# Window attention with sink columns and two feed-forward layers on one core: operands arranged on the host, transposes left out, small products on GpSimd, stages reordered

## The chip, the cores and the metric

The kernel runs on one NeuronCore of a Trainium2 chip. The metric is device time in microseconds (us) of one execution. Engines are named as in the profile: PE (TensorE matmuls), PEld (its weight loads), DVE (VectorE), ACT (ScalarE), POOL (GpSimd) and SP (SyncE, which issues the loads and stores).

## The reference, cut

```python
scores = 0.125 * q @ k.T                 # B=2, H=8, S=768, D=64
keep   = (pos_k < n_sink) | (0 <= pos_q - pos_k < window)     # 4 sinks, window 128
a      = softmax(where(keep, scores, -1e9))
x      = (a @ v) as [1536, 512]
x      = ((x @ w_a) * (x @ w_b)) @ w_out        # d_ff 1536
y      = relu(x @ w_in2)**2 @ w_out2            # d_ff 2048
```

The feed-forward weights are float64 and reach the kernel as pairs of 32-bit words. The kernel keeps nearly float32 precision in the large products: each operand is split into a high and a low part, and a product is three matmuls (high·high, low·high, high·low).

## The kernel before, in words

**Attention** works on 24 groups g: batch b (2), block i of 128 queries (6), and half m of the heads (4 heads). A group needs the key block of its own position, the one before, and 8 sink columns. `attention_fast` is a software pipeline: in step g of its main loop each stage named in the list `ORDER` runs for group g plus the stage's lag, so one step touches up to five groups. Inside that loop the instructions stay in the order in which they are written on PE, DVE, ACT and POOL (`manual_schedule`), so `ORDER` is the order of every engine's queue. The stages, with the lines where they issue:

- `pt`, `kq`: PE transposes two key and two query tiles of the next group (L233), ACT copies them out of PSUM (L239), POOL copies the sink columns of a first block (L241).
- `scores`: 4 matmuls (L258, written as 8 instructions in the profile).
- `soft0`, `soft1`: DVE picks the right key block (L271) and adds the mask with a running minimum (L274), two heads each; `exp0`, `exp1`: ACT's exponentials with their sums (L282).
- `rec`: DVE's sum and reciprocal (L287, L288), which begin a step's chain. `norm`: DVE scales heads 0 and 1 (L292); `normA`: ACT scales heads 2 and 3 (L297).
- `sp`: DVE writes the scaled sink columns three times (L305); `pst`: PE turns them (L336); `st`: ACT copies (L342); `sts`: DVE forms the low part of the middle copy (L347).
- `ptp`, `th`: PE turns the four heads' weights (L312), ACT copies (L316); `lu`: POOL cuts them into two triangles (L327, L329).
- `x`: 16 value matmuls and 2 for the sinks (L355, L360); `xh`, `xl`: ACT and DVE write the high and low parts (L368, L371).

**Weights.** `Weights.stages` loads one 512 KB piece (L537) and decodes it in six stages on ACT and DVE (L552 to L570): `abs`, `ts`, `stt`, `stt2`, `cast`, `lo`. The list `DECODE` says in which steps a piece begins; eleven pieces are decoded beside the attention.

**Feed-forward.** `Beside` gives PE one piece of 12 matmuls (L660, 128x512) per step through the stage `fill`, from the step in which the first 512 tokens are done. After the last step come the rest of these pieces, then blocks of 512 tokens through the remaining phases (L660 and the second product, L701), with the weight pieces decoded beside them.

**Loads.** SP issues keys and queries two groups ahead, values one group later, weight pieces as raw buffers come free (3). Sinks' values are loaded once by 24 transfers (L211) into a cleared weight buffer, and split by ACT and DVE (L216, L217) at the end of step 2 (`SINK`). `warm` runs 14 small matmuls at the start and 4 and 3 more in steps 0 and 1 (L380).

Of the kernel before, what the change touches and what calls it, by code (L numbers as in the profile page):

```python
# [28 lines left out]
    ("rec", -1), ("x", -3), ("th", -2), ("sp", -1), ("norm", -1), ("scores", 0), ("pt", 1), ("xh", -3),  # L29
    ("normA", -1), ("xl", -3), ("fm", 0), ("soft0", 0), ("fu", 0), ("stt2", -1), ("soft1", 0), ("abs", 0),  # L30
    ("pst", -1), ("kq", 1), ("st", -1), ("fill", 0), ("exp0", 0), ("sts", -1), ("ts", 0), ("cast", -1), ("stt",
    0), ("lu", -2), ("lo", -1), ("exp1", 0), ("ptp", -1)]
DECODE = [2, 6, 9, 10, 11, 12, 13, 15, 18, 20, 22]
WIDE = 9
SINK = (1, 2)
PINNED = 3
WARM0 = 14
WARM1 = {0: 4, 1: 3}
NV, NEX, NTH, NLU, NSP = 8, 3, 2, 2, 2
# [22 lines left out]
def setup(tc, cp, tp, n_sink, window):  # L62
    nc = tc.nc
    c = Attn()
    ident = tp.tile([P, P], F32, name="ident")
    make_identity(nc, ident)
    c.identr = cp.tile([P, P], F32R, name="identr")
    nc.vector.tensor_copy(c.identr, ident)
    c.ident = c.identr.bitcast(F32)

    raw = cp.tile([1, 4], I32, name="raw")
    nc.scalar.dma_start(raw[:, 0:2], n_sink.bitcast(I32).partition_broadcast(1))
    nc.scalar.dma_start(raw[:, 2:4], window.bitcast(I32).partition_broadcast(1))
# [12 lines left out]
    c.up = cp.tile([P, P], I32, name="upi")  # L86
    v.tensor_copy(c.up, c.upf)
# [3 lines left out]
    c.rel0 = tp.tile([P, P], F32, name="rel0")  # L91
    v.scalar_tensor_tensor(out=c.rel0, in0=c.upf, scalar=BIG, in1=d, op0=ALU.mult, op1=ALU.add)
    lo = cp.tile([1, 2], F32, name="lo_f")
    hi = cp.tile([1, 2], F32, name="hi_f")
    v.tensor_copy(lo, raw.bitcast(U32)[:, 0:4:2])
    v.tensor_copy(hi, raw[:, 1:4:2])
    c.par0 = cp.tile([1, 2], F32, name="par0")
    v.scalar_tensor_tensor(out=c.par0, in0=hi, scalar=4294967296.0, in1=lo, op0=ALU.mult, op1=ALU.add)
    return c


def masks(tc, cp, tp, c, ps):
# [13 lines left out]
    def out_of(o, x, limit):  # L116
        v.tensor_scalar(out=o, in0=x, scalar1=limit, scalar2=-BIG, op0=ALU.is_ge, op1=ALU.mult)


    sink = tp.tile([P, P], F32, name="sink")  # L120
    out_of(sink, c.col, c.ns)
    out_of(m0, c.rel0, c.w)
    v.tensor_tensor(out=m0, in0=m0, in1=sink, op=ALU.max)

    out_of(m2[:, 0:P], c.rel, c.w)
    v.tensor_copy(m2[:, P:SW], sink[:, 0:SK])
# [4 lines left out]
    v.tensor_copy(m1[:, P:SW], sink[:, 0:SK])  # L131
# [14 lines left out]
def attention_fast(tc, ctx, c, cp, tp, rp, q, k, v, xh, xl, beside):  # L146
# [3 lines left out]
    B, H, S, D = q.shape  # L150
    NB = S // P
# [707 lines left out]
```

## Time and profile before

| what | value |
|---|---|
| median of 3 runs | 676.22 us (676.17 to 676.25) |
| the profiled execution | 678.09 us, span of its instructions 676.4 us |
| busy, share of the span | PE 96%, PEld 78%, DVE 59%, ACT 43%, POOL 4% |
| granted TensorE clock, mean | 0.986 |
| packets of loads and stores | 65,560, of which 39,908 under 512 bytes |
| HBM read, written | 45.19 MB, 3.15 MB |

The span runs from the first to the last instruction of one profiled execution. The page cuts it into 40 slices; the chain of waits says what was waited for last; the timeline lists instructions in order of time, with the idle time before each and what ended it. Matmuls are pipelined: a matmul's duration overlaps the next one, so PE's pace is read from starts. A granted clock of 1.00 is 2.4 GHz, 0.50 is 1.2 GHz.

### The profile page before, as it was taken

To read this page: it belongs to the slowest core of one execution; us is meant where nothing else is said; L and a number is where in the kernel's file an instruction comes from. 1 tells how busy PE (TensorE), PEld (TensorE's weight loads), DVE (VectorE), ACT (ScalarE), POOL (GpSimd) and SP (SyncE) were. 2 spreads that over 40 slices of the span, in tenths; PEclk is the share of its full clock that TensorE was granted. 3 is DMA by queue.
4 is the path that set the end of the run, shared out by engine and by line. 5 is a ranking of instruction groups with operands and counts; after the bars stand their busy time and mean duration, and the time that the engine had idled before them with its cause. 6 is when DMAs were issued, how large, how long until landed. Compare 5 with 4: busy or idle time off the path is not lost.

```text
span 676.4 us, 8976 instructions
## 1 busy us (share of the span) xinstructions
PE 652.0 (96%) x3267; PEld 528.6 (78%) x3267; DVE 401.7 (59%) x950; ACT 290.7 (43%) x676; POOL 30.2 (4%) x53
## 2 busy tenths in 40 slices
PE   7578999999999999999999999999999999999996
PEld 5356877778788888888888888888888888888884
DVE  5698986762689872588641789535824232333323
ACT  6676886761444532545321446324532222222221
POOL 1131202120000000000000000000000000000000
PEclk9697999999999999999999999999999999999999
DMA  5853543310164550045400043200200000001011
GB/s 136 197 121 85 145 123 85 85 33 0 63 188 133 165 169 1 32 150 162 155 1 0 32 125 125 94 0 32 63 0 1 0 1 0 1 1 62 23 40 68
DMA packets 65560, 48.99 MB, mean 72 GB/s; under 512 B 39908, under 2 KB 60388, under 8 KB 65508
## 3 DMA queue, kind: packets, MB, share of 16 engines
q1 hardware_dynamic: 65504, 48.34, 24.8%
q8 instruction: 27, 0.44, 0.3%
q14 instruction: 25, 0.20, 0.1%
q10 hardware_dynamic: 4, 0.00, 0.0%
HBM read 45.19 MB, written 3.15 MB: 71 GB/s over the span
## 4 chain that ended last, share of the span: by engine, by line
PE 92%; DVE 4%; ACT 1%; DMA 1%; SPq 1%; issue 0%; DVEq 0%; ACTq 0%
PE psa L660 48%; PE acc L701 34%; PE x L355 3%; PE sc L258 3%; PE pt L233 1%; PE ptp L312 1%; ACT ex L282 1%; PE x L360 1%; DMA qraw<-in_q_dram 1%; SPq L211 1%; DVE ex L274 1%; DVE ex L292 1%; DVE sc L271 1%; PE psw L380 1%; DVE xl L371 0%
## 5 line engine op out<-in xcount | busy, mean ns | idle before, releaser
L660 PE MATMUL psa<-xh,wh 128*128 128x512 f32 x480 | 188.9, 393 | 0.8 <-DVE gs L677 0.8
L660 PE MATMUL psa<-xh,wl 128*128 128x512 f32 x480 | 187.0, 390 | 0.0
L660 PE MATMUL psa<-xl,wh 128*128 128x512 f32 x480 | 186.8, 389 | 0.0
L660 PEld LDWEIGHTS psa<-xh,wh 128*128 128x128 f32 x480 | 90.4, 188 | 19.8 <-DVE gs L677 1.3
L660 PEld LDWEIGHTS psa<-xh,wl 128*128 128x128 f32 x480 | 90.1, 188 | 19.0
L660 PEld LDWEIGHTS psa<-xl,wh 128*128 128x128 f32 x480 | 90.3, 188 | 18.3
L740 DVE TENSOR_TENSOR g<-u 128x512 f32<-128x512 f32 x48 | 33.1, 690 | 111.2 <-ACT u L730 111.2
L730 ACT ACTIVATE u<-psa 128x512 f32<-128x512 f32 x48 | 28.7, 598 | 119.0 <-PE psa L660 119.0
L701 PE MATMUL acc<-wh,gl 128*128 128x512 f32 x192 | 74.7, 389 | 0.0
L701 PE MATMUL acc<-wl,gh 128*128 128x512 f32 x192 | 74.7, 389 | 0.0
L58 ACT CAST gh<-g 128x512 fp32r<-128x512 f32 x72 | 44.6, 620 | 64.7 <-DVE g L740 34.8
L552 ACT ACTIVATE wtmp<-wraw 128x512 f32<-128x512 f32 x68 | 45.5, 672 | 54.0 <-DMA wraw<-in_moe_w_in_dram 17.9
L59 DVE TENSOR_TENSOR gl<-g,gh 128x512 fp32r<-128x512 f32 x72 | 49.6, 689 | 31.2 <-ACT gh L58 30.9
L701 PE MATMUL acc<-wh,gh 128*128 128x512 f32 x192 | 62.7, 389 | 0.0
L568 ACT CAST wh<-wtmp 128x512 fp32r<-128x512 f32 x68 | 41.8, 618 | 35.5 <-DVE wtmp L563 15.5
L570 DVE TENSOR_TENSOR wl<-wtmp,wh 128x512 fp32r<-128x512 f32 x68 | 46.5, 685 | 17.0 <-ACT wh L568 15.9
L701 PE MATMUL acc<-gl,wh 128*128 128x512 f32 x144 | 56.0, 389 | 0.0
L701 PE MATMUL acc<-gh,wl 128*128 128x512 f32 x144 | 55.9, 389 | 0.0
L560 DVE SCALAR_TENSOR_TENSOR wtmp<-wraw,wtmp 128x512 int32<-128x512 int32 x68 | 47.4, 699 | 0.6
L701 PE MATMUL acc<-gh,wh 128*128 128x512 f32 x144 | 47.3, 389 | 0.0
L563 DVE SCALAR_TENSOR_TENSOR wtmp<-wraw,wtmp 128x512 int32<-128x512 int32 x68 | 46.5, 684 | 0.2
L701 PEld LDWEIGHTS acc<-wl,gh 128*128 128x128 f32 x192 | 36.1, 188 | 7.5
(92 smaller groups left out, 753.4 us busy)
## 6 DMA issues: line engine op xcount, KB each, us to landing
wraw<-in_moe_w_out_dram SPq DMA_DIRECT2D x28, 512.0 KB
wraw<-in_moe_w_in_dram SPq DMA_DIRECT2D x16, 512.0 KB
wraw<-in_moe_w_a_dram SPq DMA_DIRECT2D x12, 512.0 KB
wraw<-in_moe_w_b_dram SPq DMA_DIRECT2D x12, 512.0 KB
vraw<-in_v_dram SPq DMA_DIRECT2D x24, 128.0 KB
out_dram<-part SPq DMA_DIRECT2D x12, 256.0 KB
kraw<-in_k_dram SPq DMA_DIRECT2D x23, 128.0 KB
qraw<-in_q_dram SPq DMA_DIRECT2D x23, 128.0 KB
```

The costliest lines, as they stand in the source:

```text
L58: nc.scalar.copy(hi, src)
L59: (lo_eng or nc.vector).tensor_sub(lo, src, hi.bitcast(F32))
L258: nc.tensor.matmul(o, lhsT=half(flat, r)[:, qp, 0:P], rhs=y, start=True, stop=True)
L552: a = nc.scalar.activation(tf, up.bitcast(F32), AF.Abs)
L560: nc.vector.scalar_tensor_tensor(out=t, in0=up, scalar=0x3FFFFFFF, in1=t, op0=ALU.bitwise_or, op1=ALU.bitwise_and)
L563: nc.vector.scalar_tensor_tensor(out=t, in0=low, scalar=29, in1=t, op0=ALU.logical_shift_right, op1=ALU.bitwise_or)
L568: nc.scalar.copy(hi, tf)
L570: nc.vector.tensor_sub(lo, tf, hi.bitcast(F32))
L660: self.tc.nc.tensor.matmul(ps, lhsT=w[:, kt, :], rhs=x[:, kt, ts], start=n == 0, stop=n == 3 * KT - 1)
L701: mm = nc.tensor.matmul(acc[d], lhsT=a, rhs=b_, start=f == 0 and j == 0, stop=f == NF - 1 and j == 2)
L730: nc.scalar.activation(u, pa, AF.Relu)
L740: nc.vector.tensor_mul(g, u, u)
```

## The change

1. A new function `layout` rearranges inputs on the host: keys and queries come transposed, with the 8 sink keys appended to every key block; values come with all heads of a block together; the sinks' values arrive as one array `vs`; `n_sink` and `window` arrive repeated for 128 partitions; each weight piece is one contiguous block.
2. The stages `pt`, `kq` and `sts` are gone with their 96 transposes and 24 copies. Keys and queries of a block (all 8 heads) are loaded every second step.
3. `norm` scales head 0 on DVE, `normA` heads 1 and 2 on ACT, a new `normP` head 3 on POOL. `sp` is three POOL instructions: scale, round into two of three copies, difference into the third.
4. The sinks' values come in one transfer per batch, split at the end of steps 3 and 6 (`VS`). The masks need no matmul; those not used by a first block are made at the end of step 0 (`later_masks`). The warming matmuls of steps 0 and 1 are gone.
5. `ORDER` is new; of its stages, `x` now stands behind `scores`, `xl` behind `fill`. In `DECODE` the second and seventh pieces begin one step earlier.

```diff
-DECODE = [2, 6, 9, 10, 11, 12, 13, 15, 18, 20, 22]
+    ("exp1", -1), ("scores", 0), ("st", -2), ("rec", -1), ("fm", 0), ("stt", -1), ("norm", -1), ("th", -2),
...
+DECODE = [2, 5, 9, 10, 11, 12, 12, 15, 18, 20, 22]
...
-SINK = (1, 2)
+VS = (3, 6)
...
-WARM1 = {0: 4, 1: 3}
...
+    raw = cp.tile([P, 4], I32, name="raw")
+    nc.scalar.dma_start(raw, span.bitcast(I32))
...
-    nc.tensor.matmul(ps, lhsT=c.one, rhs=c.par0, start=True, stop=True)
...
+    keys = p1.tile([P, NK, H // 2, SW], F32, name="keys")
...
+    def load_kq(n, part=slice(0, H // 2)):
...
+            queries[n] = p2.tile([P, H // 2, P], F32, name="queries", tag="queries", bufs=NQ)
+        b, i = divmod(n, NB)
+        nc.sync.dma_start(keys[:, n % NK, part], k[b, i, :, part])
+        nc.sync.dma_start(queries[n][:, part], q[b, i, :, part])
...
+    with tc.high_priority(offset=1000):
+        load_kq(0, slice(0, 2))
+        load_kq(0, slice(2, 4))
+    load_kq(1)
+    load_v(0)
...
-        nc.gpsimd.memset(vsr, 0.0)
-        for kind in range(3):
-            for j in range(GH):
-                for b in range(B):
-                    p0 = (kind * GH + j) * SK
-                    nc.sync.dma_start(vsr[p0:p0 + SK, b, j // 2:H // 2:2, (j % 2) * D:(j % 2 + 1) * D],
-                                      v[b, j:H:GH, 0:SK, :].rearrange("m s d -> s m d"))
...
+    def sink_load(b):
+        vsr[b] = p1.tile([96, H // 2, P], F32, name="vsr", tag="vsr")
+        nc.sync.dma_start(vsr[b], vs_in[:, b])
...
-                nc.tensor.transpose(pt[:, j, pp], t[:, 2 * pp:2 * pp + 2, :].rearrange("t h d -> t (h d)"), c.ident)
...
-        nc.scalar.copy(kq[:, ks:qs + 1:qs - ks, :, 0:P], pts.pop(g))
...
-        nc.vector.tensor_mul(ex[:, 0:2, 0:P], ex[:, 0:2, 0:P], ss[:, 0:2].unsqueeze(2).to_broadcast([P, 2, P]))
...
+        nc.vector.tensor_scalar_mul(ex[:, 0, 0:P], ex[:, 0, 0:P], ss[:, 0:1])
...
+    def normalize_p(g):
+        ex, ss = pns[g][0:2]
+        for h in range(3, 4):
+            nc.gpsimd.tensor_scalar_mul(ex[:, h, 0:P], ex[:, h, 0:P], ss[:, h:h + 1])
...
+        sn = ex[:, :, P:SW]
+        sps[g] = sp = p2.tile([P, 3, GH, SK], F32R, name="sp", tag="sp", bufs=NSP)
+        nc.gpsimd.tensor_mul(sn, sn, ss.unsqueeze(2).to_broadcast([P, GH, SK]))
+        nc.gpsimd.tensor_copy(sp[:, 0:3:2], sn.unsqueeze(1).to_broadcast([P, 2, GH, SK]))
+        nc.gpsimd.tensor_sub(sp[:, 1], sn, sp[:, 0].bitcast(F32))
...
-        nc.vector.tensor_sub(sts[g][32:64], sps.pop((g, "t"))[32:64], sts[g][32:64].bitcast(F32))
...
+        if g == 0:
+            later_masks(tc, cp, tp, c)
             flag(tc, cp, c)
-            sink_split()
+        if g in VS:
+            sink_split(VS.index(g))
+            if g == VS[0]:
+                sink_load(1)
...
-            self.tc.nc.sync.dma_start(raw.rearrange("p (k f) t -> p k (f t)", k=src.shape[1]), src)
+            self.tc.nc.sync.dma_start(raw.rearrange("p n t -> p (n t)"), src)
```

DVE's queue, one step without weight stages, before the first feed-forward piece. `ss` holds the sums, `sc` the scores in PSUM, `ex` the exponentials. Before:

```order
L287 TENSOR_SCALAR ss<-ss 128x4
L288 RECIPROCAL ss<-ss 128x4
L305 TENSOR_TENSOR sp<-ex,ss 128x96
L292 TENSOR_TENSOR ex<-ex,ss 128x2x128
L371 TENSOR_TENSOR xl<-x,xh 128x2x128
L271 COPY_PREDICATED sc<-upi,sc 128x2x128
...
L274 ISA nb 128x1
L347 TENSOR_TENSOR st<-pst,st 32x128
```

With the change:

```order
L254 TENSOR_SCALAR ss<-ss 128x4
L255 RECIPROCAL ss<-ss 128x4
L259 TENSOR_SCALAR ex<-ex,ss 128x128
L238 COPY_PREDICATED sc<-upi,sc 128x2x128
...
L241 ISA nb 128x1
L340 TENSOR_TENSOR xl<-x,xh 128x2x128
```

The sink product, the difference and one of two heads have left the queue, and `xl` moved behind the two softmax stages.

POOL's queue in such a step; `th` holds the turned weights, `lu` their two triangles. Before:

```order
L327 AFFINE_SELECT lu<-th 128x512
L329 AFFINE_SELECT lu<-th 128x512
```

With the change:

```order
L278 TENSOR_TENSOR ex<-ex,ss 128x4x8
L279 CAST sp<-ex 128x2x32
L280 TENSOR_TENSOR sp<-ex,sp 128x32
L269 TENSOR_SCALAR ex<-ex,ss 128x128
L301 AFFINE_SELECT lu<-th 128x512
L303 AFFINE_SELECT lu<-th 128x512
```

Four short instructions of the group whose sums have just been formed now stand ahead of the two selects.

PE's queue in such a step (`pst` the turned sink columns, `ptp` the turned weights). Before:

```order
L312 MATMUL ptp<-identr,ex 128x128 x4
L355 MATMUL x<-lu,vraw 64x128 x8
L360 MATMUL x<-st,vs 128x128 x2
L258 MATMUL sc<-kq 128x272 x4
L233 MATMUL pt<-identr,kraw 128x128 x2
L233 MATMUL pt<-identr,qraw 128x128 x2
L336 MATMUL pst<-identr,sp 96x128
```

With the change:

```order
L286 MATMUL ptp<-identr,ex 128x128 x4
L225 MATMUL sc<-keys,queries 128x272 x4
L324 MATMUL x<-lu,values 64x128 x8
L329 MATMUL x<-st,vs 128x128 x2
L310 MATMUL pst<-identr,sp 96x128
```

The four transposes are gone and the scores stand ahead of the value matmuls. The first piece of 12 feed-forward matmuls stood behind `pst` of group 9, in step 10; it now stands behind `pst` of group 10, in step 11.

## Rows read from the trace of the kernel before

**Rows 1.** Windows: stretch; busy PE, PEld, DVE, ACT, POOL; granted clock, DMA share, GB/s.

```profile
5.00:10.00 5.00, 4.18 (x34) 3.05 (x33) 2.99 (x19) 2.71 (x10) 1.30 (x3) 1.00 1.03 216
...
17.00:20.00 3.00, 0.00 (x0) 0.00 (x0) 0.54 (x6) 0.00 (x0) 0.00 (x0) 0.86 0.06 14
20.00:23.00 3.00, 0.00 (x0) 0.00 (x0) 1.17 (x2) 1.82 (x4) 0.00 (x0) 0.50 0.48 106
...
100.00:120.00 20.00, 20.00 (x146) 15.65 (x145) 14.68 (x61) 14.37 (x51) 3.89 (x6) 1.00 0.38 94
```

**Rows 2.** Chain that ended last, in order of time: start, duration, engine, what.

```profile
103.75 1.12 PE sc L258 x8
105.56 2.77 PE psa L660 x12
...
110.17 1.12 PE sc L258 x8
```

**Rows 3.** Timeline, DVE: `rec` of groups 0, 2, 3, 9; start, duration, instruction.

```profile
9.64 0.17 DVE L287 TENSOR_SCALAR ss<-ss 128x4 f32<-128x4 f32 x1 [1.17 <-ACT ex L282]
...
23.14 0.17 DVE L287 TENSOR_SCALAR ss<-ss 128x4 f32<-128x4 f32 x1
...
27.84 0.16 DVE L287 TENSOR_SCALAR ss<-ss 128x4 f32<-128x4 f32 x1
...
59.22 0.59 DVE L287 TENSOR_SCALAR ss<-ss 128x4 f32<-128x4 f32 x1
```

**Rows 4.** Timeline, SP and ACT: the sinks' load and split.

```profile
9.45 10.79 SPq L211 DMA_DIRECT2D wraw<-in_v_dram  x24
...
21.18 1.14 ACT L216 CAST vs<-wraw 96x512 fp32r<-96x512 f32 x2 [4.53 <-DMA wraw<-in_v_dram]
```

**Rows 5.** Timeline, PE's weight loads: the wait for the last of the first transfers.

```profile
4.69 0.18 PEld L233 LDWEIGHTS pt<-identr,qraw 128*128 128x128 f32 x1 [0.21 <-DMA qraw<-in_q_dram]
```

**Rows 6.** Groups of instructions by line: busy us, mean ns, idle before.

```profile
L560 DVE SCALAR_TENSOR_TENSOR wtmp<-wraw,wtmp 128x512 int32<-128x512 int32 x68 | 47.4, 699 | 0.6
...
L556 DVE TENSOR_SCALAR wtmp<-wtmp 128x512 f32<-128x512 f32 x68 | 29.1, 431 | 17.6 <-ACT wtmp L552 16.8
...
L239 ACT COPY kq<-pt 128x512 f32<-128x512 f32 x24 | 13.9, 578 | 8.8 <-PE pt L233 8.7
...
L241 POOL COPY kq<-kq 128x32 f32<-128x32 f32 x4 | 1.2, 306 | 21.6 <-ACT kq L239 21.6
...
L85 DVE TENSOR_SCALAR up<-d 128x128 f32<-128x128 f32 x1 | 0.2, 232 | 0.2 <-POOL d L81 0.2
```

**Rows 7.** Timeline, DVE: one step of the front without weight stages.

```profile
37.09 0.17 DVE L287 TENSOR_SCALAR ss<-ss 128x4 f32<-128x4 f32 x1 [0.42 <-ACT ex L282]
...
37.50 0.26 DVE L305 TENSOR_TENSOR sp<-ex,ss 128x96 f32<-128x96 f32 x1
37.68 0.85 DVE L292 TENSOR_TENSOR ex<-ex,ss 128x256 f32<-128x256 f32 x1
...
40.82 0.28 DVE L347 TENSOR_TENSOR st<-pst,st 32x128 fp32r<-32x128 f32 x1
```

**Rows 8.** Timeline: a POOL select beside that product, and the product alone.

```profile
37.59 0.66 POOL L327 TENSOR_SCALAR_AFFINE_SELECT lu<-th 128x512 f32<-128x512 f32 x1 [3.01 <-ACT th L316]
...
102.74 0.42 DVE L292 TENSOR_TENSOR ex<-ex,ss 128x256 f32<-128x256 f32 x1
```

**Rows 9.** Timeline, PE: values and scores at the low clock, first feed-forward piece, transposes.

```profile
57.34 1.97 PE L355 MATMUL x<-lu,vraw 128*64 128x128 f32 x16 [1.12 <-DVE st L347]
...
59.87 2.19 PE L258 MATMUL sc<-kq 64*128 64x272 f32 x8
...
62.96 0.74 PE L660 MATMUL psa<-xh,wh 128*128 128x512 f32 x1
...
104.79 0.44 PE L233 MATMUL pt<-identr,kraw 128*128 128x128 f32 x2
...
105.29 0.27 PE L336 MATMUL pst<-identr,sp 128*96 128x128 f32 x1
```

More of the change, by code (lines that the diff above doesn't have):

```diff
@@ L28 @@
 ORDER = [
[L29 to L32, printed above, removed]
-DECODE = [2, 6, 9, 10, 11, 12, 13, 15, 18, 20, 22]
[4 rows of a table added]
+DECODE = [2, 5, 9, 10, 11, 12, 12, 15, 18, 20, 22]
 WIDE = 9
-SINK = (1, 2)
+VS = (3, 6)
 PINNED = 3
 WARM0 = 14
-WARM1 = {0: 4, 1: 3}
-NV, NEX, NTH, NLU, NSP = 8, 3, 2, 2, 2
+NQ, NV, NEX, NTH, NLU, NSP = 3, 5, 3, 2, 2, 2
+NK = 4
 T = 512
@@ L214, in sink_split @@
-    def sink_split():
-        for b in range(B):
-            nc.scalar.copy(vs[:, b], vsr[:, b])
-            nc.vector.tensor_sub(vs[64:96, b], vsr[64:96, b], vs[64:96, b].bitcast(F32))
-    kq = p1.tile([P, 6, 2, SW], F32, name="kq")
-    flat = kq.rearrange("p a c s -> p (a c) s")
+    pns, ths, sps, sts, lus, xs = ({} for _ in range(6))
+    keys = p1.tile([P, NK, H // 2, SW], F32, name="keys")
+    queries, vals = {}, {}
+    def load_kq(n, part=slice(0, H // 2)):
+        if n >= B * NB:
+            return
+        if n not in queries:
+            queries[n] = p2.tile([P, H // 2, P], F32, name="queries", tag="queries", bufs=NQ)
+        b, i = divmod(n, NB)
+        nc.sync.dma_start(keys[:, n % NK, part], k[b, i, :, part])
+        nc.sync.dma_start(queries[n][:, part], q[b, i, :, part])
@@ L224, in half, with sink_split @@
+    def sink_split(b):
+        nc.scalar.copy(vs[:, b], vsr[b])
+        nc.vector.tensor_sub(vs[64:96, b], vsr[b][64:96], vs[64:96, b].bitcast(F32))
     def half(t, r):
         return t[r * D:(r + 1) * D]
[L227 to L234 removed]
@@ L257, in scores @@
                     o = sc[:, r, 0:2 * SW].rearrange("q (u s) -> q u s", u=2)
-                nc.tensor.matmul(o, lhsT=half(flat, r)[:, qp, 0:P], rhs=y, start=True, stop=True)
+                nc.tensor.matmul(o, lhsT=half(queries[n], r)[:, 2 * m + pp], rhs=y, start=True, stop=True)
     def maxima(g, pp):
@@ L384, in attention_fast @@
                   soft1=lambda g: maxima(g, 1), exp0=lambda g: exps(g, 0), exp1=lambda g: exps(g, 1), rec=reciprocal,
-                  norm=normalize, normA=normalize_too, sp=sinks, pst=sinks_turn, st=sinks_copy, sts=sinks_low, pt=transposes, kq=transposes_copy,
-                  x=values, xh=x_high, xl=x_low)
+                  sp=sinks, pst=sinks_turn, st=sinks_copy, x=values, xh=x_high, xl=x_low,
+                  norm=normalize, normA=normalize_a, normP=normalize_p)
     warm(WARM0)
-    transposes(0)
-    masks(tc, cp, tp, c, bank("par")[:, 0, 0:2])
-    transposes_copy(0)
     for g in range(N + 3):
@@ L843, in build, with layout, pairs, blocks @@
     return nc
+def layout(inputs):
+    import numpy as np
+    def pairs(a, n):
+        B, H, S, D = a.shape
+        a = a.reshape(B, H // 2, 2, S // n, n, D).transpose(0, 3, 2, 5, 1, 4)
+        return a.reshape(B, S // n, 2 * D, H // 2, n)
+    def blocks(w, inner):
+        if inner:
+            K, FF = w.shape
+            w = w.reshape(K // P, P, FF // P, P).transpose(2, 1, 0, 3)
+        return np.ascontiguousarray(w.reshape(-1, P, 512)).view(np.int64)
+    q, k, v = (np.asarray(inputs[n]) for n in "qkv")
+    B, H, S, D = v.shape
+    out = {"q": pairs(q, P)}
+    sinks = pairs(k[:, :, 0:SK], SK)
+    out["k"] = np.concatenate([pairs(k, P), np.broadcast_to(sinks, (B, S // P, *sinks.shape[2:]))], axis=4)
+    out["v"] = v.reshape(B, H, S // P, P, D).transpose(0, 2, 3, 1, 4)
+    vs = np.zeros((3, 4, SK, B, H // 4, 2, 2, D), v.dtype)
+    for j in range(4):
+        vs[:, j, :, :, :, j // 2, j % 2] = v[:, j::4, 0:SK].transpose(2, 0, 1, 3)
+    out["vs"] = vs.reshape(12 * SK, B, H // 2, 2 * D)
+    out["span"] = np.broadcast_to(np.stack([inputs["n_sink"], inputs["window"]]).astype(np.int64), (P, 2))
+    for n in _INS[5:]:
+        out[n] = blocks(np.asarray(inputs[n]), not n.endswith("out"))
+    return out
 def kernel(**inputs):
@@ L849 @@
     from concourse.bass_utils import run_bass_kernel_spmd as _run
+    inputs = layout(inputs)
     arrays, shapes = {}, {}
```

210 lines of the change are left out of this document (76 added, 134 removed), and 3 rows, old and new, of the table ORDER.

## The prediction

> **What bounds the kernel now.** First come the windows, which cut the span into stretches by what each engine did. From the first feed-forward piece at 62.96 us [rows 9] on, PE works without a pause worth naming: 20.00 of 20 us in the stretch 100 to 120, at the full clock, with DVE and ACT at about 14.5 of 20 [rows 1]. There the chain of waits has nothing but PE's own work, step after step, from one group's scores at 103.75 to the next one's at 110.17 [rows 2], 6.42 us. So time from 62.96 to the end of the span at 676.4, 613.4 us, is a count of PE's work, and only work that leaves PE shortens it. Before 62.96 PE is not the bound: from 17 to 23 it did nothing [rows 1]. There the timeline of DVE is the thing to read, by its first instruction of each step, the `rec` of one group (group 0 at 9.64, 2 at 23.14, 3 at 27.84, 9 at 59.22) [rows 3]. I therefore sum two parts: when the first piece starts, and what PE has left then.
>
> **Part one, the front.** *Step 0.* PE waits for the last of the first four transfers until 4.69 [rows 5]. They carry 256 KB before and 553 KB now, since a block's keys and queries hold all 8 heads. At the 216 GB/s of the stretch 5 to 10 [rows 1] the extra 297 KB cost 1.4 us, so the second half lands at 6.1; scores 0.4 and two softmax instructions 0.5 bring DVE to 7.0. No transposes and no copy come between. But the later masks and the flags, some eleven small instructions, now stand ahead of `rec` of group 0: at 0.17 [rows 3] to 0.23 each [rows 6], 1.9 to 2.5 us; I take 2.0, since most write few columns. `rec` of group 0: 9.0 instead of 9.64 (bounds 7.5, if the longer transfers run faster, and 9.8).
>
> *Steps 1 and 2.* Before, `rec` of group 2 comes 13.50 us after that of group 0. Six of these, 17 to 23, are the sinks' wait: DVE did the flags (0.54) and the split (1.17) and was idle otherwise [rows 1], because 24 small transfers held SP for 10.79 us and ACT waited 4.53 for them [rows 4]. All six leave these steps. ACT's two copies of 0.578 [rows 6], on the chain here, go too: 13.50 - 6.0 - 1.1 = 6.4, so 15.4.
>
> *A step without weight stages.* DVE is busy from `rec` at 37.09 to the end of `sts` at 41.10, 4.01 us, after 0.42 idle [rows 7]. Out go the sink product (0.18, start to start), the difference (0.28), and of the norm's 0.85 all but one head, which at 0.232 for 128x128 [rows 6] leaves 0.6 saved: 1.06 to 1.1 in all, or 2.9 left. `xl` behind `soft1` covers part of the wait for ACT's exponentials, but with less DVE work that wait grows to about 0.7: 3.6 a step. ACT loses only its copy; PE needs x, scores, sinks and `ptp`, some 3.3. So three engines then stand close together, and I expect no more than this. A weight piece adds two instructions of 0.43 to one step and three of 0.70 [rows 6] to the next: 0.9 and 2.1 (the first fills the wait).
>
> *The sum.* Step 3, with the second half of a piece and a sinks' split of 0.6 to 0.7: 2.9 + 2.1 + 0.6 = 5.6, `rec` of group 3 at 21.0. From group 3 to group 9 it took 31.4 before [rows 3]; now 3.6 + 3.9 + 5.6 + 3.6 + 3.6 + 3.9 = 24.2, and 0.8 for collisions with POOL (below): 25.0, at 46.0. Step 10 carries one piece's second half and the next one's first: 2.9 + 2.1 + 0.9 = 5.9, at 51.9. The first piece now stands in step 11, a step later than before, because `xl` of group 7 falls behind `fill` in step 10. It comes behind `pst` of group 10, which waits for POOL's three new instructions: 0.3 each by POOL's 128x32 copy of 0.306 [rows 6], so 1.4 behind `rec`. First piece: 53.3.
>
> *The clock.* After the six idle microseconds the clock in the rows stood at 0.50 from 20 to 23 [rows 1]; scores then take 2.19 instead of about 1.15 [rows 2, 9]. The change removes that pause, but also the warming matmuls and the transposes, and leaves PE about 4 us of work between 4 and 13. One stretch at 1.2 GHz there is likely; the long step 3 hides most of it. I take 2.0 (0 to 6). **First piece at 55.3 instead of 62.96** (bounds 50 and 61).
>
> **Part two, PE's remaining work.** In each of steps 11 to 22 four transposes go, 0.50 from their start to `pst`'s [rows 9]: 12 x 0.50 = 6.0. Since the first piece starts a step later, one step's attention work more is already done: 6.42 - 2.75 for the piece - 0.50 = 3.2. Against that, weight stages crowd on DVE, since `DECODE` begins two pieces in step 12. Step 11: 2.9 + 2.1 + 0.9. Steps 12 and 13 serve first blocks, whose two key choices fall away (0.9, if each is as long as the 0.43 of [rows 6]): 2.0 + 2.1 + 1.8, and 2.0 + 4.2 with a feed-forward product of 0.7. With 0.3 a step for collisions that is 6.2, 6.2 and 7.2, where PE has 5.9: 1.9 us in which PE waits (0 to 6). 613.4 - 6.0 - 3.2 + 1.9 = 606.1. Everything after the attention is the same PE work. **Span 55.3 + 606.1 = 661.4.** The profiled execution took 678.1 with a span of 676.4, its median is 676.2; I take the 15.0 off the median: **661.2 us.**
>
> **What is costed at nothing.** Longer, fewer loads: PE's stretches after 63 show no wait for them, so they help only the front. The contiguous weight pieces likewise. ACT's copy beyond step 2: ACT is not the bound there. POOL was idle for 3.01 us before its select at 37.59 [rows 8]; the four new instructions, 1.2 us by the copy's 0.306, fit into that. If they took as long as a select, 0.66 [rows 8], POOL would have 3.9 a step and be as late as DVE: this is the upper bound, and it costs the front 0.3 a step.
>
> The copy's 0.306 is the nearest row for POOL, a one-input instruction; two of the new ones have two inputs, and no row shows that on POOL. The Trainium skill ("GPSIMD Engine Reference", section "Engine selection") speaks against this move: elementwise work on VectorE, since two-input operations are about twice as slow on GpSimd. By that rule the product and the difference would take about 0.6 each as an estimate, `pst` would come 0.6 later, and the sum would be 661.8 instead of 661.2.
>
> **The rivals.** *The port takes it back.* A DVE product beside a POOL select took 0.85 [rows 7, 8], alone 0.42 [rows 8]. Each new POOL instruction can meet a two-input DVE instruction so. Two more such meetings in each of about nine front steps cost 2 x 0.43 x 9 = 7.7: 669. For it: POOL's busy time per step doubles. Against it: what stays on DVE reads mostly PSUM, and the norm is a single head. The Trainium skill ("Perfetto Trace Analysis", section "Optimizing Scalar/DVE Operations") warns of this: the two engines share a port, so moving work between them might not help. Chance 0.13.
>
> *POOL becomes the bound, slower than before.* Say every step takes y because POOL does. The first piece then comes at 9.0 + 10 y + 1.4, and each of the 15 steps behind it costs y - 5.9 more, while DVE's 1.9 no longer counts. All of the 15.0 is lost when 25 y = 15.0 + 55.3 - 10.4 + 88.5 + 1.9, at y = 6.0. POOL's two selects are 1.3 of that [rows 8], so from 1.2 us for each new instruction on this decides; at 1.3 each, y is 6.5 and the time 676.2 + 25 x 0.5 = 689. The point is an instruction on 32 to 128 columns that takes four times the copy's 0.306. Chance 0.04.
>
> *PE stays at 1.2 GHz through the front.* At that clock values 1.97 and scores 2.19 [rows 9], and the sinks, `pst` and `ptp` about 2, make 6.1 a step: PE is the bound from group 3 at 21.0, seven such steps and 5.0 to the first piece, 68.7 instead of 55.3: 674.6. Against it: PE would then work without a pause, as it does from 100 to 120, where the clock is 1.00 [rows 1], so some of the seven steps would be fast; with four slow ones it is 669. Chance 0.04.
>
> *Better than forecast.* No low clock, faster first loads, no wait in steps 11 to 13: 50 + 604.2, less 0.2, is 654. Chance 0.09.
>
> **How the numbers follow.** The forecast, DVE's queue shortened and PE counted down, 655 to 667, has 0.70. The range 655 to 669 takes it in with the larger part of the port case and leaves out the end of the good case, the clock case's last third and POOL's. A measurement of this kernel tells 0.2% from no change. Only POOL's case is slower (0.04); what it gives near its point, with the clock case at its full price, is the same (0.02); the others are faster: 0.94.
>
> **What would show it.** In the changed profile: `rec` of group 2 by about 15.4 with no pause behind the sinks' load; DVE's plain step 3.6 long; the first feed-forward piece near 55; then PE full, in steps of 5.9 us. It would be wrong if the first piece stood later than 61, if POOL ended a step's last wait (its new instructions above 1.1 us), or if PE paused between pieces for weights.

## The result and the profile after

The changed kernel takes **658.76 us** (median of four runs, 658.13 to 660.43) against 676.24 in the same comparison: ratio 0.9745, interval [0.9727, 0.9763], or 17.2 us faster. The forecast was 661.2 in a range of 655 to 669. The profiled execution, the longest of the four, took 660.43 us with a span of 658.7; the rows below are from it.

The two parts of the sum share the gain: the first feed-forward piece stands at 54.11 us instead of 62.96 [rows 9], 8.9 earlier, and from there to the end it takes 604.6 us instead of 613.4, 8.8 less.

The windows of the changed kernel (stretch; busy PE, PEld, DVE, ACT, POOL; granted clock, DMA share, GB/s) answer to [rows 1]:

```profile
5.00:10.00 5.00, 2.86 (x20) 1.90 (x20) 3.84 (x30) 3.70 (x18) 0.61 (x1) 0.90 1.01 329
...
20.00:25.00 5.00, 4.30 (x24) 2.72 (x21) 4.22 (x20) 4.47 (x19) 2.74 (x7) 0.50 0.50 183
...
100.00:120.00 20.00, 20.00 (x146) 15.52 (x146) 15.96 (x60) 14.60 (x53) 8.99 (x22) 1.00 0.17 54
160.00:180.00 20.00, 18.21 (x81) 15.06 (x81) 18.13 (x35) 9.28 (x16) 0.00 (x0) 1.00 0.45 150
```

The pause of 17 to 23 is gone: DVE and ACT are busy for over four of the five microseconds from 20 to 25. Transfers move at 329 GB/s in 5 to 10, where it was 216. From 100 to 120 PE still has no pause, and POOL has 8.99 where it had 3.89. But in two of these stretches something is lost: the clock is 0.50 from 20 to 25, and PE has 1.79 us of pause in 160 to 180.

DVE's timeline, `rec` of groups 0 to 5, 9 and 10, answers to [rows 3]:

```profile
7.47 0.16 DVE L254 TENSOR_SCALAR ss<-ss 128x4 f32<-128x4 f32 x1
10.21 0.17 DVE L254 TENSOR_SCALAR ss<-ss 128x4 f32<-128x4 f32 x1 [1.20 <-ACT ex L249]
15.49 0.17 DVE L254 TENSOR_SCALAR ss<-ss 128x4 f32<-128x4 f32 x1 [0.68 <-ACT ex L249]
20.84 0.17 DVE L254 TENSOR_SCALAR ss<-ss 128x4 f32<-128x4 f32 x1
24.20 0.17 DVE L254 TENSOR_SCALAR ss<-ss 128x4 f32<-128x4 f32 x1 [0.40 <-ACT ex L249]
29.26 0.17 DVE L254 TENSOR_SCALAR ss<-ss 128x4 f32<-128x4 f32 x1 [0.35 <-ACT ex L249]
...
45.40 0.16 DVE L254 TENSOR_SCALAR ss<-ss 128x4 f32<-128x4 f32 x1
50.71 0.16 DVE L254 TENSOR_SCALAR ss<-ss 128x4 f32<-128x4 f32 x1
```

Two steps are longer than the forecast has them: the one from group 1 to group 2 lasts 5.28 us (8.02 from group 0, not 6.4), and the one from group 4 to group 5 lasts 5.06, not 3.9. What held the first is in SP's and ACT's timelines:

```profile
5.98 0.59 SPq L496 DMA_DIRECT2D wraw<-in_moe_w_a_dram  x1
...
13.22 0.68 ACT L511 ACTIVATE wtmp<-wraw 128x512 f32<-128x512 f32 x1 [1.83 <-DMA wraw<-in_moe_w_a_dram]
```

The first weight piece is issued at 5.98, as the twelfth load, and ACT waits 1.83 us for it, with the exponentials of group 2 queued behind `abs`. What held the second, and what stands ahead of the first piece, is in PE's and ACT's timelines (they answer to [rows 9]; the last three rows are a saturated step):

```profile
23.48 2.19 PE L225 MATMUL sc<-keys,queries 64*128 64x272 f32 x8
25.59 1.29 PE L324 MATMUL x<-lu,values 128*64 128x128 f32 x16
27.29 0.37 ACT L337 CAST xh<-x 128x256 fp32r<-128x256 f32 x1 [1.34 <-PE x L329]
...
49.46 0.70 PE L286 MATMUL ptp<-identr,ex 128*128 128x128 f32 x4 [1.56 <-DVE xl L340]
50.09 2.19 PE L225 MATMUL sc<-keys,queries 64*128 64x272 f32 x8
52.21 1.63 PE L324 MATMUL x<-lu,values 128*64 128x128 f32 x16
...
54.11 0.47 PE L619 MATMUL psa<-xh,wh 128*128 128x512 f32 x1
...
101.73 1.19 PE L225 MATMUL sc<-keys,queries 64*128 64x272 f32 x8
...
104.15 0.23 PE L310 MATMUL pst<-identr,sp 128*96 128x128 f32 x1
...
107.59 1.19 PE L225 MATMUL sc<-keys,queries 64*128 64x272 f32 x8
```

Twice the scores take 2.19 us, at the low clock, instead of 1.19. The values stand behind them now, so they come late; ACT's `xh` then waits 1.34 for them, and the exponentials wait behind `xh`. A saturated step lasts 107.59 - 101.73 = 5.86 us instead of 6.42 [rows 2].

POOL's timeline, the three sink instructions and the head's norm, first with little beside them; then the cast beside a weight decode on DVE, whose row stands above it:

```profile
24.75 0.24 POOL L278 TENSOR_TENSOR ex<-ex,ss 128x32 f32<-128x32 f32 x1 [0.71 <-DVE ss L255]
25.06 0.24 POOL L279 CAST sp<-ex 128x64 fp32r<-128x64 f32 x1
25.38 0.25 POOL L280 TENSOR_TENSOR sp<-ex,sp 128x32 fp32r<-128x32 f32 x1
25.61 0.60 POOL L269 TENSOR_SCALAR ex<-ex,ss 128x128 f32<-128x128 f32 x1
...
51.78 0.69 DVE L522 SCALAR_TENSOR_TENSOR wtmp<-wraw,wtmp 128x512 int32<-128x512 int32 x1
51.83 0.73 POOL L279 CAST sp<-ex 128x64 fp32r<-128x64 f32 x1
```

The pause behind the attention is PE's row at 161.87, from the list of waits along PE's timeline:

```profile
161.87 0.47 PE L619 MATMUL psa<-xh,wh 128*128 128x512 f32 x1 [1.79 <-DVE gs L636]
```

ACT had the product's input, `u`, done at 158.0, but DVE's queue has six decode instructions of three weight pieces ahead of `gs`: they start at 158.63 to 160.71, the first after 1.25 us of waiting for ACT, and `gs` follows at 161.04 (DVE's timeline).

### The profile page after: what moved, and what is told of

It is laid out like the page before. It is cut to its first block, busy times and chain, and to the rows that moved or that the text cites. A ratio compares the mean times of both kernels' runs of the same rounds, so it can differ in the third digit from the quotient of the medians.

```text
span 658.7 us, 8703 instructions
## 1 busy us (share of the span) xinstructions
PE 638.1 (97%) x3162; PEld 515.9 (78%) x3162; DVE 384.5 (58%) x908; ACT 279.1 (42%) x652; POOL 59.7 (9%) x132
## 2 busy tenths in 40 slices
DMA packets 17411, 49.47 MB, mean 75 GB/s; under 512 B 2064, under 2 KB 2576, under 8 KB 17360
## 4 chain that ended last, share of the span: by engine, by line
PE 84%; DVE 6%; DMA 4%; ACT 2%; issue 1%; POOL 1%; SPq 1%; POOLq 0%; ACTq 0%; DVEq 0%
PE psa L619 45%; PE acc L660 31%; DMA wraw<-in_moe_w_a_dram 3%; PE sc L225 3%; PE x L324 3%; DMA wraw<-in_moe_w_out_dram 1%; PE ptp L286 1%; DVE wtmp L522 1%; DVE wtmp L519 1%; PE x L329 1%; ACT wtmp L511 1%; ACT ex L249 1%; DVE ex L241 1%; DVE wl L529 1%; DVE gl L59 1%
```

## The experiments

Twelve kernels ran, in three groups, each against the kernel before on the same chip (its medians: 677.36, 676.82 and 678.10). As these differ by over 1 us, ratios are compared; 0.001 is 0.68 us. The changed kernel's is 0.9745 [0.9727, 0.9763]. The last column is read from one execution of each kernel; in which steps the clock is low differs among these (see `e10`), and such a step counts about 1.2 us.

| run | median us | ratio, interval | first piece |
|---|---|---|---|
| e1_no_gpsimd | 673.97 | 0.9957 [0.9940, 0.9975] | 61.07 |
| e2_transposes_back | 666.89 | 0.9855 [0.9837, 0.9872] | 52.89 |
| e3_before_sinks | 673.83 | 0.9955 [0.9936, 0.9975] | 59.04 |
| e4_old_order | 661.96 | 0.9772 [0.9751, 0.9792] | 52.49, a step earlier |
| e5_no_gpsimd_early | 673.18 | 0.9945 [0.9926, 0.9965] | 60.48 |
| e6_weight_first | 658.59 | 0.9733 [0.9717, 0.9750] | 51.88 |
| e7_head_pace | 659.28 | 0.9735 [0.9719, 0.9752] | 54.48 |
| e8_xl_before_fill | 657.07 | 0.9709 [0.9692, 0.9726] | 48.68, a step earlier |
| e9_three_edits | 656.61 | 0.9686 [0.9669, 0.9702] | 47.07, a step earlier |
| e10_norm_on_vector | 660.84 | 0.9750 [0.9732, 0.9768] | 53.34 |
| e11_weights_strided | 662.69 | 0.9777 [0.9757, 0.9796] | 52.15 |
| e12_warm_front | 658.72 | 0.9721 [0.9702, 0.9740] | 52.27 |

**Is it the GpSimd move?** The first run undoes it in the changed kernel.

```diff
-        nc.vector.tensor_scalar_mul(ex[:, 0, 0:P], ex[:, 0, 0:P], ss[:, 0:1])
+        nc.vector.tensor_mul(ex[:, 0:2, 0:P], ex[:, 0:2, 0:P], ss[:, 0:2].unsqueeze(2).to_broadcast([P, 2, P]))
...
-        nc.gpsimd.tensor_mul(sn, sn, ss.unsqueeze(2).to_broadcast([P, GH, SK]))
-        nc.gpsimd.tensor_copy(sp[:, 0:3:2], sn.unsqueeze(1).to_broadcast([P, 2, GH, SK]))
-        nc.gpsimd.tensor_sub(sp[:, 1], sn, sp[:, 0].bitcast(F32))
+        nc.vector.tensor_mul(sps[g], ex[:, :, P:SW].unsqueeze(1).to_broadcast([P, 3, GH, SK]),
+                             ss.unsqueeze(1).unsqueeze(3).to_broadcast([P, 3, GH, SK]))
...
+        nc.vector.tensor_sub(sts[g][32:64], sps.pop((g, "t"))[32:64], sts[g][32:64].bitcast(F32))
```

> The changed kernel with the move to GpSimd undone: the sink product (three copies), the low part of its middle copy and the norm of two heads stand on VectorE again, the norm of the other two on ScalarE; layout, loads and the order of the other stages stay as changed. Theory (VectorE's queue sets the front, PE's work the rest): VectorE gets 0.7 to 0.8 us a step back, the first feed-forward piece comes at 59 to 61 instead of 54.1, the steps behind it stay as long, time 664 to 667. Rival (the port takes back what leaves VectorE, or ScalarE and PE set the front): first piece at 53 to 56, time 658 to 660.

Both were too low: 673.97, a ratio 0.0212 above the changed kernel's, or 14.3 us. The first piece comes 7.0 later, and from 47 us on PE pauses 7.9 us in eight waits of `pst` for the product (5.6 of it in the six that lie behind the first piece), which in the new order stands late in DVE's queue. So a rival was left open, that it is the place and not the engine; `e5` puts the product straight behind `rec` (the edit against `e1`):

```diff
-    ("exp1", -1), ... ("stt", -1), ("norm", -1), ("sts", -2), ... ("x", -3), ("sp", -1), ("pst", -1),
+    ("exp1", -1), ... ("stt", -1), ("sp", -1), ("norm", -1), ("sts", -2), ... ("x", -3), ("pst", -1),
```

> As e1_no_gpsimd, but the sink product stands on VectorE straight behind the reciprocal, where the kernel before had it, and not behind the first softmax stage, where PE's turn of the sink columns and the feed-forward piece queued behind it waited for it. It tells how much of e1's 15 us is the GpSimd move and how much that place. Theory (the move is worth the 0.8 us a step of the front, and the waits behind the first piece came from the place): first piece at 60 to 61, steps behind it 5.8 to 6.0 without waits of PE, time 664 to 667. Rival (the move is worth all of it, since VectorE's longer queue delays PE behind the first piece too): 671 to 674.

673.18, which is the rival's: the place is worth 0.8 us, inside the noise, and the engine, with the form of the instructions, 13.5. The waits of PE from 47 us on show the form of it (waited for, by what: us in total, times, longest):

```profile
PE ptp L279 <- DVE xl L338: 4.6, 2, 2.7
PE x L322 <- DVE st L314: 3.6, 2, 2.3
...
```

No single instruction is waited for: PE waits twice for `xl`, behind DVE's two softmax stages, before the first piece, and twice for `st`, behind the product and the norm, after it. DVE's window shows its queue nearly full, 35.69 of 40 us, where the changed kernel has 32.05:

```profile
60.00:100.00 40.00, 37.57 (x270) 28.94 (x264) 35.69 (x130) 28.12 (x100) 6.39 (x9) 1.00 0.44 141
```

**Sinks or norm?** `e10` leaves the sinks on GpSimd and moves the head's norm back to DVE.

```diff
-            nc.gpsimd.tensor_scalar_mul(ex[:, h, 0:P], ex[:, h, 0:P], ss[:, h:h + 1])
+            nc.vector.tensor_scalar_mul(ex[:, h, 0:P], ex[:, h, 0:P], ss[:, h:h + 1])
```

> The changed kernel, but the one head's norm that GpSimd does is back on VectorE behind the other head's; the sinks' three instructions stay on GpSimd. Theory (the long cost of undoing the whole move, 14.5 us, is VectorE's queue in proportion to the busy time it gets back): the norm is about a third of it, so 663 to 665, first piece at 56 to 57 us. Rival (the cost was the sinks' product and difference, which stand between `rec` and the transposes that PE waits for, and the norm is free): 657 to 660.

The rival held, by the ratio: 0.9750 against 0.9745. DVE's timeline of one plain step shows why:

```profile
37.04 0.17 DVE L254 TENSOR_SCALAR ss<-ss 128x4 f32<-128x4 f32 x1 [0.40 <-ACT ex L249]
...
37.46 0.29 DVE L259 TENSOR_SCALAR ex<-ex,ss 128x128 f32<-128x128 f32 x1
37.66 0.28 DVE L269 TENSOR_SCALAR ex<-ex,ss 128x128 f32<-128x128 f32 x1
...
40.60 0.17 DVE L254 TENSOR_SCALAR ss<-ss 128x4 f32<-128x4 f32 x1 [0.40 <-ACT ex L249]
```

The step, `rec` at 37.04 to 40.60, lasts 3.56 us; in the changed kernel the same step (37.97 to 41.54) lasts 3.57, with a wait of 0.62 at its end. The second head's 0.2 us, start to start, goes into that slack. In `e5`, with the product, the difference and two heads on DVE, the plain step is 3.99 long (41.89 to 45.88). So it is mainly the sinks' work that had to leave DVE. How much the form of the norm adds is not shown: `e1` and `e5` do it as one two-input product of 128x256, `e10` as two scalings of 128x128. In a plain step that is 0.45 against 0.40, start to start, but where a POOL select is already under way (51.58 to 52.23 in `e5`), DVE's product takes twice as long; where the product starts first (42.48, 0.42 long), it is the select that takes 0.84 instead of 0.63 to 0.65:

```profile
42.55 0.84 POOL L294 TENSOR_SCALAR_AFFINE_SELECT lu<-th 128x512 f32<-128x512 f32 x1 [3.92 <-ACT th L283]
...
51.66 0.85 DVE L259 TENSOR_TENSOR ex<-ex,ss 128x256 f32<-128x256 f32 x1
```

`e10` also shows how far single traces can be compared. Its step from group 4 to group 5 lasts 3.85 (24.06 to 27.91), with the clock at 1.00 from 22 to 28; but its step 10 lasts 6.63 (44.46 to 51.09) instead of 5.31, since there the clock is 0.50, the values are slow and ACT's `xh` waits for them:

```profile
45.00:48.00 3.00, 3.00 (x23) 1.96 (x19) 2.82 (x11) 1.29 (x4) 2.58 (x5) 0.50 0.16 31
48.59 0.37 ACT L337 CAST xh<-x 128x256 fp32r<-128x256 f32 x1 [2.29 <-PE x L329]
```

So a first piece that comes 1 us earlier or later in one trace settles nothing, and the times of `e10` still leave the norm up to some 2 us.

**The transposes.** `e2` puts four back into each group on PE, into a PSUM bank that nothing reads, without the copies.

```diff
+            nc.tensor.transpose(pt[:, pp], keys[:, n % NK, 2 * m + pp, 0:P], c.ident)
...
+            nc.tensor.transpose(pt[:, 2 + pp], queries[n][:, 2 * m + pp], c.ident)
```

> The changed kernel with four transposes per group put back on PE alone, behind the scores; nobody reads them. Theory (behind the first piece time is a count of PE's work, in front of it PE has room): 0.5 us in each of steps 11 to 23, 6.0 to 6.5 in all, the front longer by 0 to 2 us, time 665 to 668. Rival (PE's room is there behind the first piece too, since VectorE or the weights set the pace): 659 to 661. Second rival (the extra work keeps the clock up in the front): first piece earlier than 54.1, time 663 to 665.

666.89, 0.0110 or 7.4 us more: what theory said. A saturated step in PE's timeline, from `sc` to `sc`, is 6.45 long, 0.59 above the changed kernel's:

```profile
105.17 1.19 PE L225 MATMUL sc<-keys,queries 64*128 64x272 f32 x8
106.28 0.44 PE L232 MATMUL pt<-identr,keys 128*128 128x128 f32 x2
...
111.62 1.19 PE L225 MATMUL sc<-keys,queries 64*128 64x272 f32 x8
```

Behind the first piece `e2` takes 664.7 - 52.89 = 611.8 us, 7.2 more. Yet the first piece comes 1.2 us earlier. That doesn't make the transposes free in the front: the plain step from group 7 to group 8 lasts 4.17 there (36.83 to 41.00, DVE's timeline) instead of 3.57. What comes back is clock: the step from group 4 to group 5 lasts 3.88 instead of 5.06, and the scores ahead of the first piece are fast. That is the second rival's mechanism, but `e10` and `e11` have that step fast without added work, so that the transposes keep the clock up isn't shown.

**The sinks' load.** `e3` is the kernel before with the sinks' values in one transfer.

```diff
-        for kind in range(3):
-            for j in range(GH):
-                for b in range(B):
...
+        nc.sync.dma_start(vsr, vs_in)
```

> The kernel before with one part of the change alone: the sinks' values come from the host in one transfer in place of 24 and the clearing. Theory (the stretch 17 to 23 was a wait for these transfers and for SP behind them): first piece at 56 to 58 instead of 62.96, time 669 to 671. Rival (the wait is for the bytes in front of it, keys, queries and weights, and only changes its name): 674 to 676.

673.83, or 3.0 us less, with the interval 1.7 to 4.3: less than theory said, but more than the rival. `rec` of group 2 moves from 23.14 to 18.84, 4.3 and not 6, since split and flags stay in that step, as DVE's timeline shows:

```profile
17.52 1.29 DVE L211 TENSOR_TENSOR vs<-wraw,vs 32x512 fp32r<-32x512 f32 x2
18.84 0.17 DVE L281 TENSOR_SCALAR ss<-ss 128x4 f32<-128x4 f32 x1
```

**The order.** `e4` gives the changed kernel the old `ORDER` (without the removed stages, `normP` behind `norm`) and the old `DECODE`.

```diff
-DECODE = [2, 5, 9, 10, 11, 12, 12, 15, 18, 20, 22]
+DECODE = [2, 6, 9, 10, 11, 12, 13, 15, 18, 20, 22]
```

> The changed kernel with the stages in the order of the kernel before (the removed ones left out, the new norm beside the old one) and its list of weight pieces. Theory (the sums of each engine's work set the front, the order only moves waits): first piece in step 10 again at 51 to 57, time 657 to 663. Rival (the order carries the gain: with the old one ScalarE and PE wait for GpSimd's sink chain within the step): first piece at 59 to 63, time above 665.

661.96, 0.0027 or 1.8 us above, with overlapping intervals: by their ends, at most some 4 us lie in the new order.

**The wait for the first weight piece.** `e6` asks for it at the start of step 0, ahead of the keys and queries which that step loads, and not in step 1.

```diff
+        if g == 0:
+            beside.W.load()
         if g % 2 == 0:
             load_kq(g // 2 + 2)
...
-        if step + 1 in DECODE[:2]:
+        if step + 1 in DECODE[1:2]:
```

> The changed kernel with its first weight piece asked for at the start of step 0, ahead of the third block's keys and queries, instead of in step 1 behind them. In the changed kernel ScalarE waited 1.83 us in step 2 for that piece, with the exponentials of group 2 behind it. Theory (that wait is the 1.7 us by which step 2 was longer than forecast): reciprocal of group 2 at 13.6 to 14.0 instead of 15.49, first feed-forward piece at 52 to 53, time 657 to 658. Rival (the front makes the loss up later, or keys and queries come late instead): 658.5 to 660.

The load goes out 1.9 us earlier, as the eighth, the wait of `abs` is gone (no idle time before it), and `rec` of group 2 comes at 13.31 instead of 15.49 (SP's and ACT's timelines):

```profile
4.07 0.43 SPq L498 DMA_DIRECT2D wraw<-in_moe_w_a_dram  x1
...
11.04 0.67 ACT L513 ACTIVATE wtmp<-wraw 128x512 f32<-128x512 f32 x1
```

The first piece is 2.2 us earlier in the profile, as theory said, but the time is only 0.8 less by the ratio, with overlapping intervals, and the median is the rival's. The traces are of single executions, and the changed kernel's is the longest of its four; whether all 2.2 arrive stays open.

**The wait behind the attention.** `e7` lets a decode go ahead with every second piece there, and no longer at the pace of the later pieces.

```diff
-                        W.ahead()
+                        W.ahead(2)
```

> The changed kernel with a weight piece decoded after every second feed-forward piece, instead of every third, in the stretch between the attention and the first block (124 to 160 us, where VectorE is busy for two fifths). In the changed kernel PE waited 1.79 us at 161.9 for a product that stood behind weight stages on VectorE, and the chain then goes through loads of weights. Theory (after the attention, now 21 us shorter, the weights are the next to be late): less waiting, time 657 to 658.5. Rival (that wait is the change of the PSUM pools, as in the kernel before with 0.85, and one does not get around it): 658.5 to 660.

The wait is 0.85 us instead of 1.79, but the time doesn't tell it from the changed kernel (0.9735): this cost is too small to matter alone. As the rival had it, 0.85 is left, which the kernel before has too; `e4` and `e8` come to the same without this edit.

**The wait for `xl`.** `e8` puts `xl` ahead of `fill` and `soft1`.

```diff
-    ("fu", 0), ("xh", -3), ("cast", -1), ("fill", 0), ("soft1", 0), ("xl", -3), ("lu", -2), ("ptp", -1),
+    ("fu", 0), ("xh", -3), ("cast", -1), ("xl", -3), ("fill", 0), ("soft1", 0), ("lu", -2), ("ptp", -1),
```

> The changed kernel with the low part of the value product (xl) ahead of the feed-forward piece and of the second softmax stage, so that the first piece comes in step 10 again and the PSUM buffer of the values is freed sooner for the turned weights (PE waited 2.8 us in all for it). Theory (VectorE is the front's queue: xl waits for PE's values and holds up the second softmax stage behind it): first piece 4 to 6 us earlier, but steps of the front longer by 0.3 to 0.6, time 657 to 662. Rival (the freed buffer matters more): 655 to 657.

657.07, 0.0036 or 2.4 us less, between the two expectations, and both have their part: a plain step does get longer (38.21 to 42.24, 4.03 instead of 3.57), but the buffer comes free sooner. PE's timeline: the wait for `xl` at the last step without pieces is halved, the scores behind it are fast (1.19), and the first piece stands in step 10, where it does wait for POOL:

```profile
44.76 0.66 PE L286 MATMUL ptp<-identr,ex 128*128 128x128 f32 x4 [0.77 <-DVE xl L340]
...
48.58 0.27 PE L310 MATMUL pst<-identr,sp 128*96 128x128 f32 x1 [0.51 <-POOL sp L280]
48.68 0.47 PE L619 MATMUL psa<-xh,wh 128*128 128x512 f32 x1
```

**Together.** `e9` has the edits of `e6`, `e7` and `e8`.

> The changed kernel with the edits of three earlier runs together: `xl` before `fill`, first weight piece asked for at step 0, one decode with every second feed-forward piece in the head. Theory (what comes before the first piece and the wait behind the attention add up): 1.5 us for `xl`, 0.2 to 2 for the early weight, up to 0.5 for the pace: 655 to 657, first piece before 48.7 us. Rival (the gains cancel, because the early steps are then held by another engine): 657 to 659, not to be told from the run with `xl` alone (657.07).

656.61, ratio 0.9686: 4.0 us below the changed kernel's, with intervals apart, and 21.2 below the kernel before. The time and the first piece at 47.07 are as theory said. But against `e8` the intervals overlap, so the rival isn't out.

**Contiguous weights.** `e11` leaves the weights in memory as they were; each piece is a strided load.

```diff
-            self.tc.nc.sync.dma_start(raw.rearrange("p n t -> p (n t)"), src)
+            self.tc.nc.sync.dma_start(raw.rearrange("p (k f) t -> p k (f t)", k=src.shape[1]), src)
```

> The changed kernel, but the weights lie in memory as before, so each piece is loaded in strided rows and not in one contiguous block. Theory (transfers of weights stand beside PE's work everywhere but before the first piece): 658 to 660, steps behind the first piece unchanged. Rival (the piece's longer transfer delays the decodes in step 2 and at the wait behind the attention): 661 to 664, with `rec` of group 2 over 16.5 us or the wait at `gs` over 3 us.

Not settled: the median, 662.69, is the rival's, but the runs lie between 659.19 and 663.52, and the interval overlaps the changed kernel's. In the profiled execution, the fastest of the four, nothing waits longer for weights but `abs` in step 2 (2.14 instead of 1.83), although the packets go from 17,411 to 32,771.

**The clock.** `e12` gives PE six warming matmuls in each of steps 0 to 3.

```diff
+WARM1 = {0: 6, 1: 6, 2: 6, 3: 6}
...
+        if g in WARM1:
+            warm(WARM1[g])
```

> The changed kernel with six more warming matmuls on zeros in each of steps 0 to 3, so that PE does not stand still there. Theory (the half clock in the stretch 20 to 25 costs the front 1 to 2 us): the clock in 20 to 25 rises towards 1.00, the first piece comes at 52 to 53 us and the time is 657 to 658. Rival (VectorE sets the front, and PE's low clock lies beside it): 658 to 661, first piece at 54 or later.

The granted clock is 1.00 in every stretch from 5 to 35, and the step from group 4 to 5 is 3.88 us long instead of 5.06 (DVE's and PE's timelines; the values follow at 23.63 and not at 25.59, behind fast scores):

```profile
23.53 0.17 DVE L255 TENSOR_SCALAR ss<-ss 128x4 f32<-128x4 f32 x1 [0.40 <-ACT ex L250]
23.63 1.09 PE L325 MATMUL x<-lu,values 128*64 128x128 f32 x16
...
27.41 0.16 DVE L255 TENSOR_SCALAR ss<-ss 128x4 f32<-128x4 f32 x1
```

So the low clock costs the front 1.2 us in that step, as theory said (`e10` and `e11` have it fast too, 3.85 and 3.88), and the first piece comes at 52.27. The warming holds up `rec` of group 0, to 8.75, so part is given back; the time, 658.72, is 1.6 less by the ratio, inside the interval. The other slow scores stay, at 48.35, behind the wait for `xl`; those `e8` removes.

## Why the prediction was right, point by point

The forecast's case, DVE's queue shortened and PE counted down, is what happened, and the time lies 2.4 us below it. In part that is luck: two terms of the front were off by about 1.5 us each, and cancel. The terms of the front, against DVE's rows above:

| term | forecast | measured |
|---|---|---|
| `rec` of group 0 | 9.0 | 7.47 |
| from there to group 2 | 6.4 | 8.02 |
| step 3 | 5.6 | 5.35 |
| group 3 to group 9 | 25.0 | 24.56, 1.2 of it clock |
| step 10 | 5.9 | 5.31 |
| to the first piece | 1.4, and 2.0 for the clock | 3.40, over 1 of it clock |
| first piece | 55.3 | 54.11 |

*Step 0 was mis-sized by 1.5 us.* The step "the second half lands at 6.1; scores 0.4" let group 0 wait for all of the first four transfers. Its four heads are the first part of `load_kq`, so its scores need the first two alone and start at 4.14; the second half is group 1's, whose scores wait for it till 5.89 (PE's timeline):

```profile
4.14 1.23 PE L225 MATMUL sc<-keys,queries 64*128 64x128 f32 x8
5.89 0.71 PE L225 MATMUL sc<-keys,queries 64*128 64x128 f32 x8 [0.52 <-DMA queries<-in_q_dram]
```

DVE has finished group 0's softmax at 5.9 instead of 7.0, and masks and flags take it 1.6 (5.84 to 7.47) instead of 2.0, beside ACT's exponentials. The measured 7.47 is the lower bound, which was given for another reason, faster transfers. (The four transfers carry 528 KB by the list of loads, not 553; that is worth 0.1 us of the sum.)

*The step to group 2 failed.* "6.4" subtracted the sinks' wait and took nothing as next in line; next was the first weight piece, asked for behind eleven longer loads, and ACT's queue has the exponentials behind `abs`. `e6` shows it: with the piece asked for earlier the two steps take 6.1 (7.23 to 13.31). The prediction took a whole wait out without asking what would be late next.

*The plain step was right:* 3.35 to 3.57 against 3.6 (the steps to groups 4, 7 and 8), 2.95 of it DVE's work against 2.9, with a wait of 0.40 to 0.62 for ACT at its end, against 0.7. The 0.8 for collisions with POOL in the stretch to group 9 does not show there: apart from the step with the low clock, no step is longer than its term without it. The clock took its place, which is luck again. `e10` shows that this wait is slack: a second head goes into it.

*The clock was about right in size, 2.3 against 2.0, but not in place.* The stretch that the prediction had in mind did come:

```profile
9.00:12.00 3.00, 3.00 (x14) 1.90 (x12) 1.69 (x11) 2.34 (x10) 0.63 (x1) 0.50 1.04 317
```

It cost nothing that shows: group 0 to group 2 takes 6.08 in `e6`, where the scores at 9.07 are slow, and 6.07 in `e12`, where none are. What cost time are two later stretches. The one of 20 to 25 is not hidden; it acts through the new order, with `x` behind `scores`: slow scores make late values, a late `xh`, and late exponentials behind it, 1.2 us by `e12`. The one from 50 on lengthens scores and values ahead of the first piece by 1.0 and 0.5, start to start; as POOL's `sp` was done only at 52.9, at most 1.1 of this counts.

*What stands ahead of the first piece was the wrong engine.* The forecast had `pst` wait for POOL, 1.4 behind `rec`. In fact POOL was done at 52.9 and PE was still at the scores and values of that step, since it had waited 1.56 for `xl`, which the change put behind DVE's two softmax stages, and then ran at the low clock.

*POOL.* The two small products took 0.24 and 0.25 with little beside them, the cast 0.24, near the 0.3 taken. The norm took 0.60, as the upper bound had it for every new instruction. The Trainium skill ("GPSIMD Engine Reference", section "Engine selection") has two-input operations about twice as slow on GpSimd, from which the prediction estimated 0.6 each for the product and the difference. With little beside them they took less than half of that; but three POOL instructions of 0.73 in sum replace 0.26 and 0.28 on DVE [rows 7], so GpSimd is the slower engine here, too.

*The port rival fell.* Meetings exist: the cast took 0.73 beside a decode, not 0.24. But the saturated steps stay at 5.86, and undoing the move costs 13.5 us. The Trainium skill ("Perfetto Trace Analysis", section "Optimizing Scalar/DVE Operations") warns that moving work between these two engines might not help; in this kernel `e1` and `e5` measure that it does, for the sinks, and `e10` shows no difference for the norm. The rivals with POOL as the bound, and with the low clock through the whole front, fell too: POOL's new instructions take 0.24 to 0.73, and the clock is back at 1.00 between the slow stretches.

*PE's remaining work:* 604.6 against 606.1. The transposes gave 0.56 a step, not 0.50, as `pst` too went from 0.27 [rows 9] to 0.23. The 1.9 us of pauses in steps 11 to 13 did not come: from 54 to 154 us PE has no idle row. A pause of 1.79 that no term named came at 161.87 in their place, where the kernel before had 0.85.

*What the parts are worth together.* Undone singly, GpSimd's move counts 13.5 to 14.3 us, the transposes 7.4, the order 1.8 (not told from nothing); the sinks' load counts 3.0 in the kernel before. That is over 25 for a gain of 17.2: the parts are not additive. In `e5` a saturated step is 6.17 long (`pst` at 113.63 and two steps later at 125.97), so of the 0.56 that the missing transposes free on PE only 0.25 arrives while the sinks are on DVE; and with the transposes back (`e2`) it is 6.45, no shorter than before, although the sinks are off DVE. In a saturated step each of the two needs the other. The longer loads of keys, queries and values, ACT's copies and the masks were not undone apart; what they are worth is not shown.

## What to carry to other kernels

Where several engines stand close together, price a removal by what the next engine then allows: here removing PE's work paid in full only with DVE's queue shortened too. For each wait that goes, walk the queue of the engine that waited and ask which transfer its next instruction needs, and when that is issued. An instruction that frees a buffer (`xl` with its PSUM bank) does not belong behind work that could wait.

## What the runs showed of the hardware

A one-input scaling of 128x128 on GpSimd took 0.60 us, and a two-input product of 128x32 took 0.24; on DVE the same scaling takes 0.28. GpSimd's cast took three times as long beside DVE's decode as with little beside it (0.73 and 0.24), and DVE's two-input product of 128x256 twice as long beside a GpSimd select (0.85 and 0.42). In the rows above, of two such instructions the one that started later took longer.

The clock fell to 0.50 in a stretch that followed one with 1.19 us of PE work in four, and not within it, as the first row here and the window of 20 to 25 above show:

```profile
13.00:17.00 4.00, 1.19 (x14) 0.58 (x12) 2.33 (x7) 3.66 (x13) 0.91 (x2) 1.00 1.04 400
17.00:20.00 3.00, 2.26 (x13) 1.36 (x13) 2.82 (x13) 2.55 (x9) 1.18 (x3) 0.87 0.78 216
```

So the cost of an idle PE showed in a later step, one in which PE itself hardly waited. Which step that is differs from kernel to kernel (group 4 to 5 here, step 10 in `e10`).
